# The 32 loads of k for token tiles 8 and 9, issued from ScalarE's queue and no longer from the sync engine's

## The chip, the core and the metric

The kernel runs on one core of one Trainium2 chip. Five engines work side by side and meet through semaphores: TensorE (PE; PEld is its weight load), VectorE (DVE), ScalarE (ACT), GpSimd (POOL) and the sync engine (SP), which here only starts transfers. A transfer (DMA) is started by an instruction in the queue of an engine and then moved by 16 DMA engines. The metric is device time in microseconds (us).

## What is computed

An attention within chunks of 64 tokens is followed by two two-layer networks. The last one applies a rational function between its two products.

```python
scores = np.matmul(q_c, k_c.transpose(0, 1, 2, 4, 3)) / 8     # 8 x 8 heads, 576 tokens, head size 64, chunks of 64
attn = exp(scores - max); attn = attn / (sum(attn) + 1e-9)
x = np.matmul(attn, v_c)                                      # -> 4608 tokens x 512
x = np.maximum(x @ w_in, 0) ** 2 @ w_out                      # 512 -> 2048 -> 512
h = x @ moe2_w_in
out = (a0 + a1*h + a2*h*h + a3*h*h*h) / (1 + |b0|*|h| + |b1|*h*h + 1e-6) @ moe2_w_out
```

## The kernel before

**Tiling.** The 4608 tokens are nine blocks of 512, or 36 tiles of 128. The hidden size of 2048 is 16 pieces of 128 columns. The first network is thus 144 steps (9 blocks by 16 pieces). Each step s has a first product `mm_h(s)`, an activation `act1(s)` and a second product `mm_out1(s)`. Every product is made in three matmuls of high and low parts (`mm3`, lines 271 to 273), so a step's `mm_h` is 12 matmuls of 128x512 and its `mm_out1` another 12.

**Order.** A list of events with due times is filled by `at(time, function, ...)` and written out in the order of these times. One unit of time is one step. `mm_out1(s)` is due 2.5 units after `mm_h(s)`. In between lies `act1(s)`: a Relu and a Square on ScalarE (lines 377 and 378), then the split into a high and a low part. The attention of later tiles, the loads and the preparation of the weights are put between the steps. No engine changes its order at run time.

**What holds what.** `mm_h(s)` writes its result into PSUM from a pool of two buffers (`h_p`), which some small products of the attention use too. In this stretch `mm_h(11)` takes the buffer that held `h` of step 10, and `mm_h(12)` the one that held step 11. Neither can start before the Relu of that earlier step has read its buffer. In the names below, `r_1367` is the Relu of step 10, `r_1433` that of step 11 and `r_1506` that of step 12.

**Weights.** In the first block each 512 KB piece of `w_in` or `w_out` is loaded into `st` (`w_load`, lines 208 and 212), turned into words by two operations on ScalarE (lines 219 and 221), joined on VectorE (line 227) and split into a high part (lines 181 or 183) and a low part on GpSimd (line 186). `st_1261` is piece 14 of `w_in`, `st_1331` piece 15 of `w_in`, and `st_1363` piece 11 of `w_out`, which `mm_out1(11)` needs. The late pieces share two `st` buffers, so `st_1363` can be loaded only when `st_1261` has been joined.

**Loads of q and k.** From tile 6 on, q and k come for two tiles at a time (a unit). `load_qk(u, src, nm, hp)` is called for each of four head pairs hp and issues one transfer for each quarter of 32 partitions and each run of tokens inside one batch (line 414). Unit 1 (tiles 8 and 9, tokens 1024 to 1279) crosses a batch after 128 tokens, so each call issues eight transfers of 16 KB. All transfers of the kernel are issued by SP, in one queue. VectorE then transposes the unit (line 424) and `mm_s` multiplies q and k.

**Completion semaphores.** Each transfer reports on one of eight semaphores, which the build hands out in turn over the whole program and calls `DMAHW0` to `DMAHW7`. A transfer waits, ahead of its start, for the one that had the same semaphore before it. These waits stand in the rows of the order below.

**Who does what.** `on(name, usual)` looks a name up in the table `ON` and gives the engine for "A", "V" or "G", or the usual one where the name does not stand there.

Of the kernel before, what the change touches and what calls it, by code (L numbers as in the profile page):

```python
# [21 lines left out]
NAT = 6  # L22
LAG = 2, 3
LN_SHIFT = 20
ON = {
# [57 lines left out]
def attn_moe_moe_kernel(  # L83
# [25 lines left out]
    nc = tc.nc  # L109
# [37 lines left out]
    def count(what, usual):  # L147
        return ON.get(what, usual)

    def on(what, usual):  # L150
        return engines[ON.get(what, usual)]

# [8 lines left out]
    def stage(what, key, i):  # L161
        if done.get((what, key), 0) != i:
            raise ValueError(f"{what} {key}: stage {i} out of order")
        done[what, key] = i + 1
# [11 lines left out]
    def tl(pool, shape, dt, nm, tag=None):  # L176
        return P[pool].tile(shape, dt, name=nm, tag=tag or nm)
# [214 lines left out]
    def runs(t0, n):  # L392
        done = 0
        while done < n:
            bb, ss = divmod(t0 + done, S)
            step = min(n - done, S - ss)
            yield done, step, bb, ss
            done += step
# [9 lines left out]
    def load_qk(u, src, nm, hp):  # L408
        stage(nm, u, hp)
        if hp == 0:  # L410
            T[nm, "unit", u] = tl("attn", [128, HP, UNIT // 32, 32], F32, nm, f"{nm}0")
        for Q in range(4):
            for off, n, bb, ss in runs(NAT * 128 + u * UNIT, UNIT):
                nc.sync.dma_start(  # L414
                    out=T[nm, "unit", u][32 * Q:32 * Q + 32, hp, off // 32:(off + n) // 32],
                    in_=src[bb, 2 * hp + Q // 2, ss:ss + n, 32 * (Q % 2):32 * (Q % 2) + 32]
                    .rearrange("(t r) d -> r t d", r=32),
                )
# [460 lines left out]
    for t in range(NAT, NTILE + 1, 2):  # L879
        b, i = divmod(t, TPB)  # L880
        t0 = 8.55 if b == 1 else NF * (b - 1) + ((-1.45, 5.55)[i // 2] if b == 2 else (-2.45, 5.55)[i // 2])
        last = (t - 1,) if t == NAT else (t - 2, t - 1)
        at(t0, mm_pv2, *last)
        for c in range(2):
            at(t0 + 0.1, x2_hi, c, *last)
            at(t0 + 0.1, x2_lo, c, *last)
        early.add(int(t0) - 1)
        if t == NTILE:
            break
        at(t0, a_ps, t)  # L890
        attention(t, t0)
        attention(t + 1, t0)
        u = (t - NAT) // 2
        if t + 2 < NTILE:
            for j in range(2 * HP):
                src, nm = ((q, "qs"), (k_in, "ks"))[j // HP]
                if t < 10:
                    at(t0 + 0.3 + 0.55 * j - (1.0 if b == 1 else 0), load_qk, u + 1, src, nm, j % HP)
                else:
                    at(t0 - 0.7 + 0.85 * j, load_qk, u + 1, src, nm, j % HP)  # L900
    for j in range(2 * HP):
        src, nm = ((q, "qs"), (k_in, "ks"))[j // HP]
        at(0.5 + 0.6 * j, load_qk, 0, src, nm, j % HP)
# [117 lines left out]
```

## Time and profile before

| | |
|---|---|
| Median of three runs | 1643.08 us (1642.87 to 1644.34) |
| The profiled execution | 1644.58 us, of which the span of the profile is 1642.5 us |
| TensorE busy | 1629.9 us, 99% of the span |
| VectorE, ScalarE, GpSimd busy | 1098.0, 924.2 and 358.6 us |
| TensorE's granted clock | 1.00 over the span |

The span runs from the first to the last instruction of the profile; the time of an execution also has what lies around it, 2.1 us here. Instructions that issue transfers are not counted as busy, so SP has no row among the engines.

### The profile page before, as it was taken

What the parts mean: (1) busy time and instruction counts of PE and PEld (TensorE: products, weight loads), DVE (VectorE), ACT (ScalarE), POOL (GpSimd) and SP (SyncE); (2) the same over time, 40 slices, a digit from 0 to 9 for tenths busy, and PEclk for the clock granted to TensorE, in tenths of its full rate; (3) what the DMA queues carried; (4) which work ended last, traced back from release to release, by engine and by line L of the source; (5) the groups of instructions that cost most, each with busy time, mean ns of one, the idle gap of its engine ahead of it and who ended that gap; (6) DMA issues with size and microseconds to landing.
All of it is one profiled execution on the core that took longest, in us unless ns stands there. A gap on an engine that the chain in (4) does not pass through costs nothing.

```text
span 1642.5 us, 24430 instructions
## 1 busy us (share of the span) xinstructions
PE 1629.9 (99%) x9360; PEld 1349.2 (82%) x9360; DVE 1098.0 (67%) x1796; ACT 924.2 (56%) x1494; POOL 358.6 (22%) x290
## 2 busy tenths in 40 slices
PE   8999999999999999999999999999999999999999
PEld 7878888888888888888888888888888888888887
DVE  6875666666555566652029787877777777877777
ACT  6853333333333333322457777777777777777776
POOL 3640000000000000000773232323222232323222
PEclk9999999999999999999999999999999999999999
DMA  9854343433434333302321000000010101010000
GB/s 256 219 137 113 73 111 83 112 76 80 101 88 115 71 102 77 87 14 66 101 83 59 26 27 26 26 19 33 1 52 1 52 0 52 1 52 1 2 25 26
DMA packets 218012, 108.56 MB, mean 66 GB/s; under 512 B 186920, under 2 KB 187176, under 8 KB 216744
## 3 DMA queue, kind: packets, MB, share of 16 engines
q1 hardware_dynamic: 217896, 107.02, 24.5%
q8 instruction: 73, 1.20, 0.3%
q14 instruction: 43, 0.35, 0.1%
HBM read 79.69 MB, written 27.26 MB: 65 GB/s over the span
## 4 chain that ended last, share of the span: by engine, by line
PE 93%; SPq 3%; DMA 2%; ACT 1%; DVE 1%; issue 1%; POOL 0%; DVEq 0%; ACTq 0%
PE acc L271 16%; PE acc L272 15%; PE acc L273 15%; PE h L272 15%; PE h L271 15%; PE h L273 15%; DMA st<-in_moe_w_in_dram 1%; PE h L478 1%; SPq L414 1%; SPq L553 1%; PE a L457 1%; SPq L403 1%; DMA ks<-in_k_dram 0%; SPq L212 0%; DMA st<-in_moe_w_out_dram 0%
## 5 line engine op out<-in xcount | busy, mean ns | idle before, releaser
L271 PE MATMUL h<-x,w 128*128 128x512 f32 (+1 forms) x1160 | 450.5, 388 | 0.3 <-POOL w L186 0.3
L272 PE MATMUL h<-x,w 128*128 128x512 f32 (+1 forms) x1160 | 449.6, 388 | 0.3 <-DVE x L186 0.3
L273 PE MATMUL h<-x,w 128*128 128x512 f32 (+1 forms) x1160 | 449.5, 388 | 0.0
L186 POOL TENSOR_TENSOR gl<-g,gh 128x512 fp32r<-128x512 f32 x141 | 181.5, 1287 | 533.3 <-ACT gh L181 533.1
L377 ACT ACTIVATE r<-h 128x512 f32<-128x512 f32 x141 | 84.1, 597 | 326.1 <-PE h L273 236.9
L271 PEld LDWEIGHTS h<-x,w 128*128 128x128 f32 x1160 | 217.8, 188 | 45.4 <-POOL w L186 0.4
L273 PEld LDWEIGHTS h<-x,w 128*128 128x128 f32 x1160 | 217.8, 188 | 44.8
L272 PEld LDWEIGHTS h<-x,w 128*128 128x128 f32 x1160 | 217.7, 188 | 44.9 <-DVE x L186 0.5
L183 DVE CAST gh<-r 128x512 fp32r<-128x512 f32 x130 | 58.6, 451 | 262.0 <-ACT r L378 251.6
L271 PE MATMUL acc<-gh,w 128*128 128x512 f32 x576 | 226.6, 393 | 2.4 <-POOL w L186 2.4
L272 PE MATMUL acc<-gl,w 128*128 128x512 f32 x576 | 224.4, 390 | 0.0
L273 PE MATMUL acc<-gh,w 128*128 128x512 f32 x576 | 224.3, 389 | 0.0
L271 PE MATMUL acc<-w,gl 128*128 128x512 f32 x575 | 223.7, 389 | 0.0
L273 PE MATMUL acc<-w,gh 128*128 128x512 f32 x575 | 223.7, 389 | 0.0
L272 PE MATMUL acc<-w,gh 128*128 128x512 f32 x575 | 223.7, 389 | 0.0
L719 DVE SCALAR_TENSOR_TENSOR t<-h,co,t 128x512 f32<-128x512 f32 (+1 forms) x145 | 123.7, 853 | 147.5 <-ACT t L718 147.0
L186 POOL TENSOR_TENSOR gl<-r,gh 128x512 fp32r<-128x512 f32 x23 | 29.7, 1293 | 593.8 <-ACT gh L181 481.8
L181 ACT ACTIVATE gh<-g 128x512 fp32r<-128x512 f32 x141 | 88.7, 629 | 81.6 <-DVE g L750 81.6
L271 PEld LDWEIGHTS acc<-gh,w 128*128 128x128 f32 x576 | 108.1, 188 | 26.7 <-POOL w L186 2.8
L717 ACT ACTIVATE h<-h 128x512 f32<-128x512 f32 (+1 forms) x145 | 86.3, 595 | 72.0 <-PE h L273 71.8
L273 PEld LDWEIGHTS acc<-gh,w 128*128 128x128 f32 x576 | 108.1, 188 | 22.6
L272 PEld LDWEIGHTS acc<-w,gh 128*128 128x128 f32 x575 | 108.0, 188 | 22.4
(120 smaller groups left out, 2288.5 us busy)
## 6 DMA issues: line engine op xcount, KB each, us to landing
st<-in_moe_w_in_dram SPq DMA_DIRECT2D x32, 512.0 KB, 4.9
st<-in_moe_w_out_dram SPq DMA_DIRECT2D x32, 512.0 KB, 4.2
x2d<-ev SPq DMA_DIRECT2D x36, 256.0 KB, 3.2
x<-x2d SPq DMA_DIRECT2D x9, 1024.0 KB, 4.7
out_dram<-ev SPq DMA_DIRECT2D x35, 256.0 KB, 2.1
w2d<-wc SPq DMA_DIRECT2D x32, 256.0 KB, 2.1
w<-w2d SPq DMA_DIRECT2D x32, 256.0 KB, 2.6
v<-in_v_dram SPq DMA_DIRECT2D x28, 256.0 KB, 4.2
```

The lines of the kernel that those rows point to most:

```text
L181: nc.scalar.activation(out=o, in_=x, func=ACTF.Copy)
L183: eng.tensor_copy(out=o, in_=x)
L186: eng.tensor_tensor(out=o, in0=x, in1=hi.bitcast(F32), op=ALU.subtract)
L271: nc.tensor.matmul(out=o, lhsT=al, rhs=bh, start=first and i == 0, stop=False)
L272: nc.tensor.matmul(out=o, lhsT=ah, rhs=bl, start=False, stop=False)
L273: nc.tensor.matmul(out=o, lhsT=ah, rhs=bh, start=False, stop=last and i == len(pairs) - 1)
L377: nc.scalar.activation(out=r, in_=ps, func=ACTF.Relu)
L403: nc.sync.dma_start(out=x[off:off + n], in_=src[bb, :, ss:ss + n, :].rearrange("h p d -> p h d"))
L414: nc.sync.dma_start(out=T[nm, "unit", u][32 * Q:32 * Q + 32, hp, off // 32:(off + n) // 32], in_=src[bb, 2 * hp + Q // 2, ss:ss + n, 32 * ...
L457: nc.tensor.matmul(out=o[half(c), h, p], lhsT=q_[half(h), p, half(c)], rhs=k_[half(h), p, half(c)], start=True, stop=True)
L717: nc.scalar.activation(out=h2, in_=ps, func=ACTF.Square)
L719: nc.vector.scalar_tensor_tensor(out=t, in0=h2, scalar=co[:, 5:6], in1=t, op0=ALU.mult, op1=ALU.add)
```

## The change

The table `ON` gets four names, one for each head pair of k of unit 1. In `load_qk` the transfer is issued by ScalarE where such a name says "A", and by SP otherwise. Nothing else is edited.

```diff
-ON = {
+ON = {"lqks10": "A", "lqks11": "A", "lqks12": "A", "lqks13": "A",
@@ load_qk
-                nc.sync.dma_start(
+                (nc.scalar if on(f"lq{nm}{u}{hp}", "") is nc.scalar else nc.sync).dma_start(
                     out=T[nm, "unit", u][32 * Q:32 * Q + 32, hp, off // 32:(off + n) // 32],
```

The order of PE, VectorE and GpSimd stays the same. On ScalarE, before the change, this is the row of work from the attention of tile 6 (`ah`) over the exponential of tile 7 and steps 10 and 11 to the words of `st_1363`:

```order
L181 ACTIVATE ah_1324<-h_1319 64x256
L518 ACTIVATE e_1328<-e_1328 128x512
L377 ACTIVATE r_1367<-h_1277 128x512
L378 ACTIVATE r_1367<-r_1367 128x512
L219 ACTIVATE wc_1395<-st_1261 128x512
L221 ACTIVATE st_1261<-st_1261 128x512
L377 ACTIVATE r_1433<-h_1398 128x512
L378 ACTIVATE r_1433<-r_1433 128x512
L219 ACTIVATE wc_1453<-st_1331 128x512
L221 ACTIVATE st_1331<-st_1331 128x512
L219 ACTIVATE wc_1484<-st_1363 128x512
L221 ACTIVATE st_1363<-st_1363 128x512
```

The four calls come in with eight transfers each. After the change, the same stretch of ScalarE from behind `ah`:

```order
L414 DMA ks_1333<-in_k_dram 32x4x32 x8
L518 ACTIVATE e_1328<-e_1328 128x512
L377 ACTIVATE r_1367<-h_1277 128x512
L378 ACTIVATE r_1367<-r_1367 128x512
L414 DMA ks_1333<-in_k_dram 32x4x32 x8
L219 ACTIVATE wc_1395<-st_1261 128x512
L221 ACTIVATE st_1261<-st_1261 128x512
L414 DMA ks_1333<-in_k_dram 32x4x32 x8
L377 ACTIVATE r_1433<-h_1398 128x512
L378 ACTIVATE r_1433<-r_1433 128x512
L219 ACTIVATE wc_1453<-st_1331 128x512
L221 ACTIVATE st_1331<-st_1331 128x512
```

The first group now stands ahead of the exponential and the Relu of step 10, the second and third ahead of the Relu of step 11; the fourth follows the last row shown, ahead of the words of `st_1363`.

On SP, the difference at the same place (`qs`, `ks` and `v` are transfers of q, k and v, `st` the loads of weights):

```order
 L414 DMA qs<-in_q_dram 32x4x32 x8
 L208 DMA st<-in_moe_w_in_dram 128x2x512
-L414 DMA ks<-in_k_dram 32x4x32 x8
-L212 DMA st<-in_moe_w_out_dram 128x1024
-L414 DMA ks<-in_k_dram 32x4x32 x8
-L212 DMA st<-in_moe_w_out_dram 128x1024 x2
-L414 DMA ks<-in_k_dram 32x4x32 x16
-L212 DMA st<-in_moe_w_out_dram 128x1024 x2
+L212 DMA st<-in_moe_w_out_dram 128x1024 x5
 L403 DMA v<-in_v_dram 128x8x64 x2
```

The five loads of `w_out` now follow the last load of `w_in` (`st_1331`) with no transfer of k between them.

The waits on the completion semaphores change with the issue. On SP, after the change, the last four of the eight transfers of q that stand between the loads of `st_1261` and `st_1331`, and the loads behind them:

```order
L414 DMA qs_1101<-in_q_dram 32x4x32 [waits DMAHW5_49]
L414 DMA qs_1101<-in_q_dram 32x4x32 [waits DMAHW7_49]
L414 DMA qs_1101<-in_q_dram 32x4x32 [waits DMAHW1_49]
L414 DMA qs_1101<-in_q_dram 32x4x32 [waits DMAHW3_49]
L208 DMA st_1331<-in_moe_w_in_dram 128x2x512 [waits DMAHW5_49,DVE_49,Activation_49]
L212 DMA st_1363<-in_moe_w_out_dram 128x1024 [waits DMAHW4_49,DMAHW0_49,DVE_49]
```

SP's transfers of q now have every second semaphore, and those between go to ScalarE's transfers of k. The four shown wait for the four transfers of q ahead of them, which have the same four semaphores. Those in turn wait for the last four transfers of ScalarE's first group. `st_1331` waits for the first of the four shown.

On ScalarE, after the change, the end of the third group and what stands behind it:

```order
L414 DMA ks_1333<-in_k_dram 32x4x32 [waits DMAHW4_49]
L414 DMA ks_1333<-in_k_dram 32x4x32 [waits DMAHW5_49]
L414 DMA ks_1333<-in_k_dram 32x4x32 [waits DMAHW6_49]
L377 ACTIVATE r_1433<-h_1398 128x512 [waits DVE_49,PE_49]
L378 ACTIVATE r_1433<-r_1433 128x512 [waits Activation_49]
L219 ACTIVATE wc_1453<-st_1331 128x512 [waits Pool_49]
```

The row that waits for `DMAHW5`, seventh of the group, waits for the load of `st_1331`, which held this semaphore before it. The words of `st_1331` stand behind it and have lost their own wait for that load.

## Rows read from the trace of the kernel before

**Rows 1.** The page, costliest groups: busy us, mean ns | idle before, releaser.

```profile
L271 PE MATMUL acc<-gh,w 128*128 128x512 f32 x576 | 226.6, 393 | 2.4 <-POOL w L186 2.4
```

**Rows 2.** Timeline of PE (start us, us, what): first matmuls of steps 11, 12; last of `mm_h(13)`, first of `mm_out1(11)`.

```profile
89.10 0.39 PE L271 MATMUL h<-x,w 128*128 128x512 f32 x1
...
95.07 0.39 PE L271 MATMUL h<-x,w 128*128 128x512 f32 x1
...
103.03 0.39 PE L273 MATMUL h<-x,w 128*128 128x512 f32 x1
105.78 0.50 PE L271 MATMUL acc<-gh,w 128*128 128x512 f32 x1 [2.36 <-POOL w L186]
```

**Rows 3.** Timeline of ACT in the stretch (in brackets: idle before, releaser).

```profile
86.57 0.38 ACT L181 ACTIVATE ah<-h 64x256 f32<-64x256 f32 x1 [0.44 <-PE h L665]
87.46 0.63 ACT L518 ACTIVATE e<-e 128x512 f32<-128x512 f32 x1 [0.52 <-DVE e L513]
88.00 0.58 ACT L377 ACTIVATE r<-h 128x512 f32<-128x512 f32 x1
...
91.43 0.67 ACT L219 ACTIVATE wc<-st 128x512 f32<-128x512 f32 x1 [2.19 <-DMA st<-in_moe_w_in_dram]
...
92.58 0.59 ACT L377 ACTIVATE r<-h 128x512 f32<-128x512 f32 x1
...
96.16 0.68 ACT L219 ACTIVATE wc<-st 128x512 f32<-128x512 f32 x1 [2.33 <-DMA st<-in_moe_w_in_dram]
...
100.96 0.66 ACT L219 ACTIVATE wc<-st 128x512 f32<-128x512 f32 x1 [3.55 <-DMA st<-in_moe_w_out_dram]
```

**Rows 4.** Timeline of SP's issues in the stretch.

```profile
87.16 0.43 SPq L208 DMA_DIRECT2D st<-in_moe_w_in_dram  x1
87.63 4.10 SPq L414 DMA_DIRECT2D qs<-in_q_dram  x8
91.85 0.39 SPq L208 DMA_DIRECT2D st<-in_moe_w_in_dram  x1
92.28 4.87 SPq L414 DMA_DIRECT2D ks<-in_k_dram  x8
97.24 0.38 SPq L212 DMA_DIRECT2D st<-in_moe_w_out_dram  x1
97.66 3.76 SPq L414 DMA_DIRECT2D ks<-in_k_dram  x8
...
103.37 8.41 SPq L414 DMA_DIRECT2D ks<-in_k_dram  x16
```

**Rows 5.** The chain of waits in order of time (start us, us, what ran or was waited for).

```profile
87.16 4.25 DMA st<-in_moe_w_in_dram
...
91.43 0.31 SPq L414
...
103.92 1.82 POOL w L186
```

**Rows 6.** Line 414 at 79.9 to 82.6 us, then its landings at 87.5 to 96.6 us.

```profile
L414 SPq DMA_DIRECT2D qs<-in_q_dram x6: 429/430/432, 79.9 to 82.3; - x6
DMA to landing us min/median/max: 1.6/1.6/1.9
...
DMA to landing us min/median/max: 1.7/2.7/3.6
```

**Rows 7.** ACT's sequencer (ACTq; ns min/median/max) and its engine, at 26 and at 948 us.

```profile
L181 ACTq EVENT_SEMAPHORE  x1: 720/720/720, 26.0 to 26.0; - x1
26.51 0.67 ACT L221 ACTIVATE st<-st 128x512 int32<-128x512 uint32 x1
...
L181 ACTq EVENT_SEMAPHORE  x1: 17/17/17, 947.8 to 947.8; - x1
947.74 0.60 ACT L717 ACTIVATE h<-h 128x512 f32<-128x512 f32 x1 [0.74 <-PE h L273]
948.81 0.78 ACT L720 ACTIVATE w<-h,co 128x512 f32<-128x512 f32 x1
```

## The prediction

> **What bounds the kernel now.** I read the page first: TensorE is busy 99% of the span, so a change pays or costs only through TensorE's waits. Its costliest groups show one wait of the size wanted in the whole run, 2.4 us ahead of a second product, released by GpSimd's split of a weight [rows 1]. PE's timeline puts it at step 11: the last matmul of the 13th first product starts at 103.03 us and the next, which needs the weight, at 105.78 [rows 2]. Rows there stand 0.23 apart, so the next was due at 103.26 and **2.5 us** are lost. The chain of waits leads from there back: the split at 103.92, ScalarE's words at 100.96, which had waited 3.55 us for their load, and that load, issued by SP at 97.24 [rows 3 to 5]. It stood behind eight transfers of k. SP goes from transfer to transfer without a pause there: eight pieces take 3.76 to 4.87 us [rows 4]. So SP's issue time holds up the weights, and it is this that the change takes off SP. The whole return is at most these 2.5 us (0.15%), since no other of the costly groups waits for a weight.
>
> The timeline of ACT shows what stands against it. Steps 10 and 11 have their Relu at 88.00 and 92.58 [rows 3], and the first products of steps 11 and 12, which reuse the two buffers, start at 89.10 and 95.07 [rows 2]. With 0.6 us for a Relu, step 10's has 0.5 us to spare and step 11's 1.9.
>
> **The change part by part.** *Price of a piece.* On SP a 16 KB piece takes 0.43 us of the queue and a pitch of 0.475 (3.76 / 8), and lands 1.6 to 1.9 us after it starts [rows 4, 6]. Among weight loads the median landing is 2.7 us [rows 6], and the densest stretch has 8.41 / 16 = 0.53 a piece [rows 4]. No row shows a transfer issued by ScalarE. I take SP's price, since it is the same instruction with the same descriptors: pitch 0.475, landing 1.9. The lower bound is a bare control instruction of ScalarE's sequencer, 0.017 us [rows 7].
>
> *What waits behind it.* The sequencer runs ahead of the engine: a semaphore instruction began at 26.0 while an activation ahead of it started only at 26.51 [rows 7]. It does not run past an activation that is still waiting: at 948, one that stands behind three activations ran only as the first of these got its input at 947.74, with the third starting at 948.81 [rows 7]. So I let ScalarE's transfers start as soon as every wait ahead of them in the queue is met, the Square's wait for its own Relu included, and let nothing behind them start before the last is issued.
>
> *The semaphores.* A transfer waits for the last holder of its semaphore. The chain shows that this is real: a piece of q waited for the weight load with the same semaphore, issued at 87.16 and landed 4.25 us later, and started at 91.43 [rows 5]. With two queues taking turns each has four of the eight, so a group's fifth piece waits for its first to land.
>
> *Group 1* starts when `ah` gets its input, 86.6. Four pieces go at 0.475; the fifth waits for the first (86.65 + 1.9 = 88.55); the eighth is issued at 90.5. The exponential (87.46 before) goes at 90.5, the Relu of step 10 ends at 91.7, and step 11's first product starts at 91.8, not 89.10: **PE waits 2.7 us**.
>
> *Group 2* starts when the Square may, at 91.7, and ends at 95.55. The words of `st_1261`, 91.43 before [rows 3], cost nothing later on.
>
> *Group 3* starts at 95.6. SP meanwhile is held: four of its pieces of q wait for group 1's fifth to eighth (landed from 90.5 on) and go at 90.5 to 92; the next four wait for those to land and go at 92.5 to 94; the load of `st_1331` waits for the first of these (92.5 + 1.9) and goes at 94.4, where it went at 91.85 [rows 4]. It lands at 94.4 + 4.25 = 98.65. The seventh piece of group 3 waits for it: 98.7, and the eighth ends at 99.65. Step 11's Relu runs from 99.65 to 100.25, and step 12's first product starts at 100.35. PE, late by 2.7, would have come there at 97.75, so **PE waits another 2.6 us** and is now 5.3 late.
>
> *Group 4* starts at 100.3. Its second piece waits for `st_1363`, which needed the joined words of `st_1261` (issue 97.6, landing 101.85); the eighth ends at 105.2. Then the words of `st_1363` run, and from their start to the second product of step 11 it was 105.78 − 100.96 = 4.82 us [rows 2, 3], with the same operations between. So that product starts at 105.2 + 4.8 = 110.0, not 105.78. PE would have been there at 103.26 + 5.3 = 108.55: **PE waits 1.5 us**, in place of 2.5.
>
> *Sum*: 2.7 + 2.6 + 1.5 − 2.5 = **+4.3 us**. SP is 15 us of issue lighter, and gains nothing: the same group of semaphores ties it to ScalarE. The pieces of k all land by 107, ahead of the 111.8 (103.37 + 8.41) at which SP ended their issue before [rows 4], so they hold nothing up. The later weights of the block are needed a step or more after `st_1363`, and I charge nothing for them; after this stretch no transfer is on ScalarE.
>
> With pitch 0.43 and landing 1.6 the same walk gives +3.3; with 0.53 and 2.7, +7.1. The granted clock stayed at 1.00 through the 2.5 us wait, and the two new waits are hardly longer, so no lower clock is charged.
>
> The Trainium skill (DMA: Bandwidth & Descriptors, section Issuing engines are not separate DMA queues) says that transfers from several engines run on the same 16 DMA engines, and that a second issuing engine saves only the sequencer's issue time, usually small beside the transfer. The trace disagrees on "small": 0.43 us of issue beside 1.6 of landing [rows 6]. By the rule the return would end at the 2.5 us that SP's issue costs.
>
> **The rivals.** *Cheap issue* (not slower): ScalarE hands a piece over at the cost of a control instruction, 0.02 to 0.06 us. The groups then take only their semaphore waits. A fifth piece still waits 1.6 us for the first, and group 3 for `st_1331`; PE loses 0.9 and 2.9 us, and the old wait shrinks by 2.5 to nothing: 3.8 − 2.5 = +1.3, so 1644.4. It decides from about 0.25 us a piece downward, where the walk gives +2.3 or less. For it speaks the 0.017 us row, against it that SP's price hardly varies. A gain over 0.2% is out of reach of this mechanism, since only 2.5 us are to be had.
>
> *Strict order*: a transfer starts only when the activation ahead of it has ended, and ScalarE is idle meanwhile. That adds the durations of words and Square at each group, some 0.6 to 1.2 us each: first products late by 3.1 and 7.2, in sum +7.0, so 1650.1. The row at 26.0 speaks against it.
>
> *One generator*: where both queues issue at once, each waits for the other's 0.43 us. This meets SP's eight pieces and group 2 (91.7 to 95.5): some six pieces of SP come between ScalarE's, 6 x 0.43 = 2.6 us, which step 11's Relu and everything behind it take over: 4.3 + 2.6 = +6.9, so 1650.0. The trace has one queue alone and cannot tell. The Trainium skill (Perfetto Trace Analysis, section DMA Instruction — HWDGE (DVE, Sync)) describes such a block, shared by two sequencers and locked by one at a time; by that rule this rival holds.
>
> *It does not do what it says*: the order shows exactly 32 transfers moved, so I give this nothing.
>
> **How the numbers follow.** The profiled execution took 1644.58 us, its span and 2.1 us around it; +4.3 makes 1648.9. It lies 1.5 above the median of the three runs, so against the median the forecast is 1643.08 + 4.3 = **1647.4 us**. Chances: the walk 0.48 (1646.4 to 1650.2), cheap issue 0.24, one generator 0.13, strict order 0.12, a gain by something unseen 0.03. The range reaches down to just below the cheap case, 1643.0, and up to 1651.3, a us above the two dear ones; outside lie the unseen gain and some of their upper ends. 0.2% (3.3 us) is about what a measurement of this kernel can tell from no change. Faster by that: 0.03. Slower: nearly all of the walk (0.41) and the two dear cases (0.25) make 0.66. The same: 0.31.
>
> **What would show it.** ScalarE's queue holds 32 transfers of about 0.43 us, in four groups of about 4 us from 86.6 to 105. PE has a wait of 2.7 us ahead of a first product at 89 and one of 2.6 at 98, both released by ScalarE's Relu, and 1.5 us remain ahead of step 11's second product. SP issues `st_1331` at about 94.4, later than before, behind pauses between its pieces of q. If ScalarE's transfers take under 0.25 us, the cheap case holds. If a transfer starts only after the activation ahead of it ends, it is strict order. If pieces take about 0.9 us where both queues issue, it is one generator. If the Relu of step 10 comes before 89, the premise that they block what stands behind is wrong.

## The result, and the profile after

The changed kernel takes **1652.88 us** (1652.03 to 1655.51, four runs) beside 1643.44 for the kernel before on the same chip: a ratio of 1.0058 (95% interval 1.0045 to 1.0071), so 9.4 us slower. 1647.4 us, 4.3 slower, was predicted, with 1651.3 as the upper end. The profiled execution took 1655.51 us, its span 1653.4.

PE's wait ahead of a second product [rows 1] has gone, and two longer waits ahead of first products have come. The page after, costliest groups (busy us, mean ns | idle before, releaser):

```profile
L271 PE MATMUL h<-x,w 128*128 128x512 f32 (+1 forms) x1160 | 453.0, 391 | 8.3 <-ACT r L377 8.0
L271 PE MATMUL acc<-gh,w 128*128 128x512 f32 x576 | 227.1, 394 | 0.0
```

PE's timeline after, the first matmuls of steps 11 and 12, which answer to [rows 2], with the next two and the last of step 12:

```profile
94.51 0.65 PE L271 MATMUL h<-x,w 128*128 128x512 f32 x1 [4.29 <-ACT r L377]
...
105.97 0.80 PE L271 MATMUL h<-x,w 128*128 128x512 f32 x1 [3.67 <-ACT r L377]
106.56 0.63 PE L272 MATMUL h<-x,w 128*128 128x512 f32 x1
106.99 0.63 PE L273 MATMUL h<-x,w 128*128 128x512 f32 x1
...
110.83 0.63 PE L273 MATMUL h<-x,w 128*128 128x512 f32 x1
```

The rows of step 12 stand 0.43 apart, where rows before stood 0.23 apart. The stretches of the trace after say why (us, busy time of PE, PEld, DVE, ACT and POOL with counts, then the granted clock, DMA share, GB/s):

```profile
94.00:95.00 1.00, 0.49 (x2) 0.39 (x3) 0.93 (x3) 0.97 (x2) 0.00 (x0) 0.85 0.19 30
95.00:96.00 1.00, 1.00 (x4) 0.81 (x3) 0.96 (x3) 0.12 (x1) 0.61 (x1) 0.50 0.33 52
...
98.00:99.00 1.00, 1.00 (x6) 0.78 (x5) 0.25 (x1) 0.75 (x2) 0.62 (x1) 0.94 1.00 138
...
105.00:106.00 1.00, 0.03 (x1) 0.03 (x1) 0.00 (x0) 0.65 (x2) 0.00 (x0) 0.50 0.22 34
106.00:108.00 2.00, 2.00 (x5) 1.62 (x6) 1.33 (x3) 1.72 (x3) 0.82 (x1) 0.50 0.16 25
...
111.00:112.00 1.00, 1.00 (x5) 0.76 (x4) 0.80 (x3) 0.94 (x3) 1.00 (x1) 0.61 0.93 357
```

Behind each wait the granted clock stood at 0.50, the 1.2 GHz level, for some 3.4 us (94.7 to 98.1) and 6.8 us (105.0 to 111.8). PE was busy for all but 1.0 us of that, so it lost half of 9.2 us, **4.6 us**. The two waits, 4.29 + 3.67, less the old 2.4, are **5.6 us**. Together they make 10.2 us, beside the 10.1 by which the way from `mm_h(9)` to `mm_h(15)` is longer (table below).

ACT's timeline after shows where the Relus stood (compare [rows 3]; ACTq rows are transfers that ScalarE's queue issued):

```profile
87.53 0.38 ACT L181 ACTIVATE ah<-h 64x256 f32<-64x256 f32 x1 [0.43 <-PE h L665]
87.61 5.69 ACTq L414 DMA_DIRECT2D ks<-in_k_dram  x8
93.34 0.63 ACT L518 ACTIVATE e<-e 128x512 f32<-128x512 f32 x1 [5.44 <-DMA ks<-in_k_dram]
93.88 0.58 ACT L377 ACTIVATE r<-h 128x512 f32<-128x512 f32 x1
94.49 0.63 ACT L378 ACTIVATE r<-r 128x512 f32<-128x512 f32 x1
94.50 3.71 ACTq L414 DMA_DIRECT2D ks<-in_k_dram  x8
...
98.31 0.87 ACTq L414 DMA_DIRECT2D ks<-in_k_dram  x2
...
99.22 6.00 ACTq L414 DMA_DIRECT2D ks<-in_k_dram  x6
105.32 0.60 ACT L377 ACTIVATE r<-h 128x512 f32<-128x512 f32 x1 [5.82 <-DMA ks<-in_k_dram]
...
110.52 0.68 ACT L219 ACTIVATE wc<-st 128x512 f32<-128x512 f32 x1 [2.80 <-POOL w L186]
```

The mechanism is the one foretold: everything behind a group waits for its last transfer. But the first group takes 5.69 us and the third 6.9, where eight at the pitch of 0.48 take 3.8. The chain of waits after (start us, us, what) names what they waited for, and SP's timeline what was under way then:

```profile
88.03 0.44 ACTq L414
...
88.51 3.96 DMA ks<-in_k_dram
...
92.49 0.32 ACTq L414
...
97.28 5.54 DMA ks<-in_k_dram
...
102.83 0.32 ACTq L414
```

```profile
88.33 0.43 SPq L208 DMA_DIRECT2D st<-in_moe_w_in_dram  x1
92.83 4.06 SPq L414 DMA_DIRECT2D qs<-in_q_dram  x8
97.00 0.38 SPq L208 DMA_DIRECT2D st<-in_moe_w_in_dram  x1
```

The third piece of group 1 was issued 0.18 us behind the 512 KB of `st_1261` and landed 3.96 us later; the seventh, which has the same semaphore, went only then. In group 2 a piece issued 0.28 us behind `st_1331` took 5.54 us, and a piece of group 3 waited for it.

### The profile page after: what moved, and what is told of

Its sections match the earlier page's. It is cut to its first block, busy times and chain, and to the rows that moved or that the text cites. A ratio compares the mean times of both kernels' runs of the same rounds, so it can differ in the third digit from the quotient of the medians.

```text
span 1653.4 us, 24430 instructions
## 1 busy us (share of the span) xinstructions
PE 1635.1 (99%) x9360; PEld 1354.0 (82%) x9360; DVE 1097.0 (66%) x1796; ACT 924.1 (56%) x1494; POOL 358.4 (22%) x290
## 4 chain that ended last, share of the span: by engine, by line
PE 97%; DMA 1%; SPq 1%; ACT 0%; ACTq 0%; DVE 0%; issue 0%; DVEq 0%
PE acc L271 16%; PE h L271 16%; PE h L272 16%; PE h L273 16%; PE acc L272 16%; PE acc L273 16%; PE h L478 1%; PE a L457 1%; SPq L553 1%; DMA ks<-in_k_dram 1%; ACTq L414 0%; DMA v<-in_v_dram 0%; PE a L432 0%; PE a L636 0%; PE h L665 0%
## 5 line engine op out<-in xcount | busy, mean ns | idle before, releaser
L272 PEld LDWEIGHTS acc<-gl,w 128*128 128x128 f32 x576 | 108.4, 188 | 22.1 <-DVE gl L186 0.3
```

The source lines that it names most:

```text
L272: nc.tensor.matmul(out=o, lhsT=ah, rhs=bl, start=False, stop=False)
```

## The experiments

In the table, the way is the time from the start of `mm_h(9)` to that of `mm_h(15)` in PE's timeline, and the extra what it has over the kernel before; it leaves out what differs between runs ahead of this stretch (the ways start between 79.5 and 83.4 us). It is read from one profiled execution of each kernel. Waits are those of PE in this stretch.

| Kernel | way, us | extra | PE waits | time over before (ratio, 95% interval) |
|---|---|---|---|---|
| before | 39.37 | | 2.4 | |
| changed | 49.44 | +10.1 | 8.0 | +9.4 (1.0045 to 1.0071) |
| g1_only | 42.08 | +2.7 | 3.6 | +3.8 (1.0011 to 1.0031) |
| g23_only | 46.39 | +7.0 | 6.6 | +6.9 (1.0029 to 1.0060) |
| g4_only | 40.51 | +1.1 | 1.9 | +2.7 (1.0003 to 1.0021) |
| behind_relu | 43.56 | +4.2 | 5.0 | +5.2 (1.0019 to 1.0038) |
| small_loads | 44.71 | +5.3 | 4.3 | +6.2 (1.0025 to 1.0052) |
| fill_clean | 47.37 | +8.0 | 1.1, and 8.6 filled | +8.9 (1.0036 to 1.0070) |
| sp_early | 38.76 | -0.6 | 1.6 | +0.5 (0.9995 to 1.0013) |
| sp_early2 | 37.53 | -1.8 | none | -1.2 (0.9985 to 1.0003) |

For the ends of the way, the first matmuls of `mm_h(9)` and `mm_h(15)` in PE's timeline before, and then after:

```profile
79.72 0.39 PE L271 MATMUL h<-x,w 128*128 128x512 f32 x1
...
119.09 0.39 PE L271 MATMUL h<-x,w 128*128 128x512 f32 x1
```

```profile
80.68 0.39 PE L271 MATMUL h<-x,w 128*128 128x512 f32 x1
...
130.12 0.39 PE L271 MATMUL h<-x,w 128*128 128x512 f32 x1
```

### One group, or two, at a time

```diff
-ON = {"lqks10": "A", "lqks11": "A", "lqks12": "A", "lqks13": "A",
+ON = {"lqks10": "A",                    # g1_only
+ON = {"lqks13": "A",                    # g4_only
+ON = {"lqks11": "A", "lqks12": "A",     # g23_only
```

> Only the first group of eight pieces of k is issued by ScalarE, the other 24 by SP. Theory A (ScalarE's queue blocks the Relu behind it): the group takes 5 to 6 us of the queue, step 11's first product waits 4 us as in the changed kernel, the second wait (step 12) is gone, the clock falls once (1.7 us), and the old wait of 2.5 us for a weight is gone: 4.3 + 1.7 - 2.5 = +3.5 us, so 1647. Theory B (the loss goes by the number of pieces on the second queue): a quarter of 9.4, +2.4 us, without any wait ahead of step 11. Theory C (only the weight load in group 3 matters): -2.5 + 0 = 1641.

> Only the fourth group is issued by ScalarE. Theory A: no Relu that TensorE waits for stands behind it (step 12's has 6 us to spare), and the load that the old wait hangs on is not ahead of it on SP, so the old 2.5 us wait stays and nothing is added: 1643.4 within 1 us. Theory B (loss by number of pieces): +2.4 us, 1645.8.

> Only the second and third group on ScalarE; the first and fourth stay on SP. Theory A, what stands behind a group waits for it and the waits overlap each other and the old one: the second group starts behind the Square of step 10 at about 88.6, the third ends at 97 to 99, so PE waits 2.5 to 4.5 us before mm_h(12), none before mm_h(11), the old wait of 2.4 us before mm_out1(11) goes, and the kernel is 0 to 4 us over the one before, the upper part of it if the clock falls after the wait. Rival, the costs of the groups add up: group 1 alone made the trace 2.7 us longer between the same two products, group 4 alone 1.1, all four 10.1, so groups 2 and 3 must cost 6.2.

Group 1 alone makes PE wait 3.61 us ahead of `mm_h(11)`, and the old wait goes, as theory A had it; the time, +3.8 us, fits too. Even the group that no first product waits for, the fourth, gains nothing: 1.91 us of the old wait stay (ahead of 109.03), with a clock of 0.57 from 110 to 114 us. Its time, +2.7 us, is the figure of theory B, but the way, +1.1, is the shorter wait and the lower clock behind it. Groups 2 and 3 cost most. The extras add to 10.8, near the 10.1 of all four, so the second expectation of g23_only was nearer: they hardly share their waits. (The times add to 13.4 beside 9.4; each is known to within some 2 us.) In g23_only PE waits once at length, 6.41 us ahead of `mm_h(12)`, and its chain shows a piece that took long with no weight load near it:

```profile
93.29 3.83 DMA ks<-in_k_dram
97.14 0.32 ACTq L414
...
98.95 3.22 DMA ks<-in_k_dram
102.18 0.61 ACT r L377
```

`st_1261` had been issued at 87.86 there and `st_1331` came at 97.38. At 93.29 SP and ScalarE were taking turns with pieces of q and k. (The piece at 98.95 does stand behind a load, 1.6 us after `st_1331`.) So a weight load is not the only thing that a piece can wait for in the DMA engines.

### Behind the Relus

```diff
-"load_qk:1,ks,0": 0.199,
+"load_qk:1,ks,0": 0.54, "load_qk:1,ks,1": 0.899, "load_qk:1,ks,2": 1.551, "load_qk:1,ks,3": 1.802,
```

> All 32 pieces still issued by ScalarE, but each group stands behind a Relu and Square instead of ahead of one (steps 10, 11, 12 and 13). Theory A (the place of the groups in ScalarE's queue is the loss): waits ahead of steps 11 and 12 fall from 8 us to under 1.5, the clock stays at 1.00, and the weights come as early or earlier than in the kernel before: 1641 to 1646. Rival (a second issuing queue costs by itself, through the semaphores or the DMA engines): +5 us or more, 1648 to 1653.

The Relus of steps 10 and 11 now come ahead of the groups. The result is about half of the loss, not none, and by its time it is the rival that came out (1650.17 us): what waits now are the words of the weights and then the second products, the next Relus and the transposes of k. PE's waits in this kernel (us in total, times, longest):

```profile
PE h L271 <- ACT r L377: 2.8, 2, 2.6
PE a L457 <- DVE k L424: 1.3, 1, 1.3
PE acc L271 <- POOL w L186: 0.7, 2, 0.5
```

So it is not the Relu alone that is short of time: in either place that was tried, 4 us of ScalarE's queue hold up something that PE needs. Of the 4.2 us on the way, the waits make 2.6 (5.0 less the old 2.4). The other 1.6 stand in no wait and in no lower clock, which was 1.00 throughout, and are not explained.

### The weight loads in flight

```diff
+        part = 8 if (n, f, half) in ((0, 14, 0), (0, 15, 0), (0, 11, 1)) else 1
...
+                out=st.rearrange("p (k f) t -> p k (f t)", k=2)[:, :, 0:1024 // part // 2],
```

> The changed kernel, but the loads of st_1261, st_1331 and st_1363 bring an eighth of their 512 KB; VectorE writes ones into the rest, so these three weights are not the reference's. In the changed kernel PE waited 4.29 us before mm_h(11) and 3.67 us before mm_h(12), and the pieces of k that were issued 0.2 to 0.3 us behind a weight load landed after 4.0 and 5.5 us. Theory A, a piece lands late because a 512 KB load is ahead of it in the DMA engines: every piece lands within 2.2 us, PE waits 2.7 +- 0.5 us before mm_h(11) and 2.4 +- 0.7 before mm_h(12), and the kernel is 3 to 6 us over the one before. Theory B, two queues that take turns make landings late whatever is in flight: landings of 4 to 5.5 us stay, the waits stay at 4.3 and 3.7, and the kernel stays 9 to 10 us over.

Theory A came out in the waits, 2.42 and 1.91 us, and nearly in the time (+6.2 us). Up to `mm_h(12)` no piece took longer than 2.1 us to land, with a median of 2.0, and group 1 took 3.82 us of the queue. The third piece, again issued just behind `st_1261`, landed in 2.1 us. The same kernel has the other case as well: a later piece, issued behind a load of `w_out` that had kept its 512 KB, took 3.5 us. SP's load and the piece behind it, twice:

```profile
88.63 0.43 SPq L209 DMA_DIRECT2D st<-in_moe_w_in_dram  x1
L420 ACTq DMA_DIRECT2D ks<-in_k_dram x1: 443/443/443, 88.8 to 88.8; - x1
DMA to landing us min/median/max: 2.1/2.1/2.1
...
106.00 0.34 SPq L213 DMA_DIRECT2D st<-in_moe_w_out_dram  x1
L420 ACTq DMA_DIRECT2D ks<-in_k_dram x1: 443/443/443, 106.4 to 106.4; - x1
DMA to landing us min/median/max: 3.5/3.5/3.5
```

So 3.7 of the 8.0 us of waits were the landings behind 512 KB loads. What is left, 2.4 and 1.9, is about what the prediction had for these two places. The way is still 5.3 us longer: 4.3 of waits less 2.4, and again a lower clock behind both (0.66 from 92 to 96 us, 0.64 from 104 to 108), which accounts for the other 3.4.

### The clock: products of zeros in the waits

To take the lower clock away without touching the waits, products of a tile of zeros were written ahead of the two first products, accumulated into a sum that they leave as it is.

```diff
+        nc.tensor.matmul(out=ACC[0][0:32], lhsT=zeros, rhs=w_slot(f, 1)[0], start=False, stop=False)
...
+    at(10.9995, fill, 16, 6)
+    at(11.9995, fill, 20, 6)
```

> The changed kernel with 16 matmuls of zeros (added to an accumulator, 3.6 us) ahead of step 11's first product and 20 (4.6 us) ahead of step 12's, where TensorE waited 4.3 and 3.7 us. Theory (the lower clock after the waits costs 4.6 us of the 9.4): the waits are filled, the granted clock stays 1.00, and step 11's and 12's products run at 0.23 us each throughout; the Relus come no earlier, so the time is 9.4 - 4.6 = +4.8 us, 1648.2. Rival (the clock in the record follows the wait and costs nothing): 1652.9 or, with the added matmuls in the way, more.

No wait was left and the clock was 1.00, but the time was 1663.64 us (ratio 1.0093 to 1.0123), far from the 1648.2 expected. The way was only 45.67 us, +6.3; the other 12 us came all over the program, where PE made fewer matmuls in the same time, as the stretches of zero_tile below show it. I took it for a price of a PE that never rests, and tested that.

> The kernel before with 11 products of zeros (about 2.6 us) written ahead of mm_out1(11), where PE waited 2.4 us. Nothing else is changed, and ScalarE issues nothing. Rival P (pace falls when PE never pauses): the products stand in the wait, yet the kernel is 8 to 12 us longer, with a pitch of about 228.5 ns over the whole rest. If instead the pace of the kernel with filled waits came from the 36 products being many, or from ScalarE's transfers, the pitch stays at 226.8 and the time is the same as before within 0.5 us.

> The changed kernel with the 20 products of zeros ahead of mm_h(12) alone; the wait of 4.3 us before mm_h(11) stays. P, it is the missing pause that slows the pace: one pause is left, the pitch stays at 226.8 ns, the lower clock after the second wait (2.9 us) goes, and the kernel is 6 to 8 us over the one before. Rival Z, products of zeros slow the pace themselves: pitch 228.5 ns over the rest, 15 us or more over.

> The changed kernel with 8 and 10 products of zeros, which leave some 2.4 us of the first wait and 1.3 of the second. P: pauses are left, the pitch stays at 226.8 ns; of the 4.5 us that the lower clock took, 0 to 3 stay, so 5.5 to 8.5 us over the kernel before. Z: pitch 228.5, 14 us or more over.

> The kernel before with 5 instead of 11 products of zeros ahead of mm_out1(11), so a pause of some 1.2 us is left of the 2.4. P: the pause that is left holds the pace at 226.8 ns and the time is that of before within 1 us. Z, or a pause of 1.2 us that is too short: pitch 228 to 228.5, 9 to 12 us over.

They ran 11.8, 19.1, 18.5 and 10.0 us over the kernel before. The rest theory seemed to hold with fill_before. It fell with fill_second and fill_part, in which PE still pauses for 4.3 and 4.9 us, and with sp_early2 (below), in which it never pauses and keeps the usual pace. Rows of fill_before stood wider already at 98 us, ahead of its first product of zeros at 104.03. What they share is the tile of zeros.

```diff
+    zeros = const.tile([128, 32], F32R, name="zeros")          # zero_tile: only this and one subtraction
...
+            pool(p1, "z", 1, side="right")                       # fill_clean: the tile in a pool of its own
```

> The kernel before with the 128-byte tile of zeros and its one subtraction on VectorE, and no product of zeros. If the tile slows the program by moving the late weights' tiles in SBUF: pitch 228.5 ns, 9 to 11 us over the kernel before. If products of zeros were the reason: pitch 226.8 and no difference.

> The changed kernel with 16 and 20 products of zeros in its two waits, the tile of zeros at the end of the other side of SBUF, where it moves no other tile. Theory clock, 4.5 us of the loss are TensorE at the lower level behind its waits: no wait and no lower clock is left, the pitch is 226.8 ns, the products take 8.7 us where the waits took 8.0, so 6.3 us over the kernel before (ratio 1.0035 to 1.004), 3 to 4 us under the changed kernel, though TensorE has no less to wait for. Rival, the lower clock only fills time that would be lost anyway: as long as the changed kernel or longer, 9 to 10 us over (ratio 1.0055 or more).

The tile alone, with no product, cost 9.4 us (ratio 1.0041 to 1.0071), although PE's old wait of 2.4 us was down to 0.3 there. (So zero_tile hardly pauses either; it is sp_early2, with no pause and the usual pace, that rules the rest theory out.) Two stretches of 200 us of zero_tile, then the same of the kernel before; the first number in brackets, behind PE's busy time, counts the matmuls:

```profile
1000.00:1200.00 200.00, 200.00 (x877) 164.25 (x876) 153.67 (x224) 149.44 (x232) 57.82 (x45) 1.00 0.07 22
1200.00:1400.00 200.00, 200.00 (x877) 164.30 (x876) 155.53 (x227) 150.06 (x233) 56.53 (x44) 1.00 0.08 32
```

```profile
1000.00:1200.00 200.00, 200.00 (x884) 165.62 (x883) 154.92 (x225) 149.97 (x234) 57.82 (x45) 1.00 0.08 27
1200.00:1400.00 200.00, 200.00 (x884) 165.58 (x884) 157.00 (x227) 151.47 (x236) 58.74 (x46) 1.00 0.07 27
```

In fill_clean, the same products with the tile elsewhere, the count is 884 again. So the fill kernels with the tile in `const` are no measure of the clock; fill_clean is:

```profile
PE h L271 <- ACT r L384: 1.1, 2, 0.8
```

```profile
90.48 3.86 PE L315 MATMUL acc<-w,zeros 128*32 128x512 f32 x16
95.16 0.50 PE L271 MATMUL h<-x,w 128*128 128x512 f32 x1 [0.82 <-ACT r L384]
101.20 4.78 PE L315 MATMUL acc<-w,zeros 128*32 128x512 f32 x20
106.28 0.50 PE L271 MATMUL h<-x,w 128*128 128x512 f32 x1 [0.29 <-ACT r L384]
```

(PE's waits of fill_clean from 36 us on, then its timeline.) The clock stays at 1.00 and the way is 8.0 us longer, between the two expectations; the time, 8.9 us over, is nearer that of the rival. The second wait, filled and not, is 4.78 + 0.29 = 5.1 us here and 3.67 in the changed kernel: there, step 11 ran at half clock in time that step 12 would have waited for anyway. So the lower clock took 4.6 us of work and cost only some of them: 10.1 − 8.0 = 2.1 us of the way. Counted from `mm_h(11)` on, ahead of which the clock was 1.00 in either kernel, it is 35.61 − 33.30 = 2.3 us, and 3.0 beside fill_waits (32.57), so 2 to 3 us by these single traces. The times of the two kernels, 9.4 and 8.9 over the one before, can't tell that from nothing: their intervals overlap.

### Another way to the 2.5 us

If SP's queue held up the late weight, the weight can be moved up in it, with the pieces of k left on SP.

```diff
-"w_load:0,11,1": -0.022,
+"w_load:0,11,1": -0.352,     # sp_early, sp_early2
-"w_load:0,12,1": -0.199,
+"w_load:0,12,1": -0.601,     # sp_early2
```

> The kernel before, all transfers on SP, but the load of st_1363 is issued ahead of the first group of k instead of behind it (the late weight is moved up the queue, the pieces of k stay where they are). It must still wait for the join of st_1261, which ended at 93.83, against an issue at 97.24 before. Theory A: it lands 3 us earlier, PE's wait of 2.4 us before mm_out1(11) is gone and nothing takes its place, so 2.4 us less than before (ratio 0.9985). Rival P, a PE that never pauses after 40 us runs at a slower pace for the rest of the program, as the kernel with filled waits did (a 128x512 product every 228.5 ns instead of 226.8): the wait goes, but the kernel is 5 to 10 us longer (1.003 to 1.006).

> The kernel before, all transfers on SP, with two late weights moved up SP's queue: st_1363 ahead of the first group of k (as in sp_early, where the wait moved to the next weight and was 1.6 us), and that next one, st of w_out piece 12, between the first and the second group. No zero products, nothing on ScalarE. Theory A: no PE wait is left, 2.4 us less than before, ratio 0.9985. Rival P, a PE without a pause after 40 us goes slower for the rest of the program: 9 to 12 us more, ratio 1.006 to 1.007, a pitch of 228.5 ns instead of 226.8, though no zero product runs.

With one weight moved, the wait went to the next one, 1.64 us ahead of 111.56. With both moved, no wait of PE is left between 36 us and the end, and the way is 1.8 us shorter. The time is 1643.44 beside 1644.67 us, a ratio of 0.9994 (0.9985 to 1.0003): the best kernel of this study, but by this measurement not shown to be faster than the one before.

## Why the prediction was wrong

*What held.* The direction and the mechanism. A transfer costs ScalarE's queue 0.44 us at a pitch of 0.48, as on SP. What stands behind a group waits for its end, ScalarE's transfers run ahead of a Square that is not done, and PE waits at the two places named, released by the Relu. Cheap issue (0.44 us, not 0.02) and strict order (group 2 began at 94.50, as the Square did) are out. So is one generator: the queues' transfers took 0.43 and 0.44 us also where both issued. The Trainium skill (Perfetto Trace Analysis, section DMA Instruction — HWDGE (DVE, Sync)) describes a block that one sequencer locks at a time; no row here shows SP and ScalarE lengthening each other's issue.

*The landing of a piece, taken at 1.9, at most 2.7.* This is the first of two steps that failed. The walk took landings from a stretch in which SP's transfers of q ran alone, and as the upper end the median of a stretch with weight loads, though the same row had 3.6 as its longest [rows 6], and a weight load itself 4.25 [rows 5]. In a chain of semaphores the longest decides, not the median: 3.96 and 5.54 us. The Trainium skill (DMA: Bandwidth & Descriptors, section Issuing engines are not separate DMA queues) says that transfers of all engines interleave on the same 16 DMA engines; the trace agrees, in that a piece of ScalarE's queue behind SP's 512 KB load landed after 3.96 us, and after 2.1 where the load was cut. While SP issued alone, a piece behind a weight load came late too (up to 3.6 us), but no compute engine stood behind it. Small_loads shows the size: 4.29 to 2.42 us at `mm_h(11)` (2.7 predicted), and 3.67 to 1.91 at `mm_h(12)` (2.6 predicted).

*`st_1331` at 94.4.* It was issued at 97.00. One us of that is this run's later start (`ah` at 87.53, 86.57 before [rows 3]); the rest is the longer group 1, for whose pieces SP's transfers of q wait. The term was right in kind and late by the same error.

*The third wait, 1.5.* It was none. The words of `st_1363` came at 110.52, 5.3 us later than in the walk, but PE was later still: only in `mm_h(12)` at that time.

*No lower clock.* This is the second step that failed, and it was wrong also at the waits that I had expected. Before, 2.36 us of wait left the clock at 1.00, as did 2.57 in behind_relu and 2.85 in fill_part (there with products of zeros ahead of the wait); in small_loads 2.42 and 1.91 us did not, nor 1.91 in g4_only. One wait without a lower clock was no ground to charge nothing. It took 4.6 us of PE's work, of which some 2 to 3 were not hidden by the second wait.

*The sum.* 4.3 predicted; the first wait is 1.6 dearer, the second 1.1, the third 1.5 cheaper, the clock adds 4.6. With the old wait at 2.4 instead of 2.5 that makes 10.2, beside 10.1 on the way. In this sum the clock stands with all it took; without it the second wait would have been longer (5.1 us in fill_clean, filled and not), so more of the loss belongs to the landings than the sum shows.

*What stays open.* Why the clock fell behind some waits of 2 to 3 us and not behind others, and what holds pieces back for 3.8 us where only small transfers are in flight (g23_only). No run gave the two queues semaphores of their own, so how much of the loss would go with that is not shown; their part in it is read from the chains of waits.

## What to carry to other kernels

A transfer in the queue of a compute engine costs that engine not only its issue time but every wait ahead of the transfer, and where completion semaphores are shared between queues that includes the slowest landing of the other queue. Price such a chain by the longest landing in the profile beside a large load, not by the median, and let the range hold a lower clock behind any new wait of TensorE of about 2 us: here the shortest wait with one was 1.91 us, and the longest without one 2.85. Moving the late transfers up in their own queue cost nothing that could be measured here (a ratio of 0.9994), where moving their neighbours to an engine in the loop cost 9.4 us.

## What the hardware showed that I had not expected

**The place of a tile.** A tile of 128 bytes a partition, added to a pool ahead of that of the late weights, cost 9.4 us: 877 matmuls in 200 us instead of 884, at a granted clock of 1.00. The wide rows come in stretches: from 100 to 130 us 128x512 products start every 231 to 233 ns in zero_tile, from 140 to 190 us every 226.6 to 227.8, as before. That it is the address of the late weights is argued from this and from fill_clean, not measured.

**When the clock falls.** In the changed kernel it went to 0.50 not in the wait but near its end: 0.2 us after PE had started again at 94.51, and 1.0 us before it started at 105.97. It stayed there for 3.4 and 6.8 us.
